# The planned delay between dependent instructions of one engine, kept for the second mixture's operations only

## The chip, the core and the metric

The kernel runs on one core of one Trainium2 chip. The metric is the device time of one execution in microseconds (us). The kernel before took 911.47 us in the median of three runs (908.46 to 913.42).

## What is computed

```python
# attention: 4 batches, 8 heads, 576 positions, head width 64, mask in blocks of 64
attn_out = _attn_ref(q, k, v)
x = attn_out.transpose(0, 2, 1, 3).reshape(2304, 512)
# first mixture
h = (x @ w1) * (x @ w2) @ w3              # 512 -> 1024 -> 1024
x = h @ w_out                             # 1024 -> 512
# second mixture
r = np.maximum(x @ w_in, 0.0)             # 512 -> 2048
return (r * r) @ w_out2                   # 2048 -> 512
```

The weights arrive as 64-bit floats and are turned into pairs of narrower numbers (a high and a low part) on the chip; each product of the mixtures is made of three products of such parts.

## The kernel before, in words

**An order worked out ahead.** The kernel doesn't issue its work as it stands in the source. Each function (`pair`, `attend`, `first_block`, `second_block`, ...) only records operations with `od.op(engine, cost, fn, reads, writes, key)`. At the end `Order.emit` (L115) plays the whole program through on paper: for each engine it holds the time at which the engine is free, and of the operations that are ready by then it takes the one with the lowest key (`min(..., key=lambda o: (o.key, o.n))`, L140). The order in which they are taken is the order of the instructions in the program. On the chip each engine then runs its list strictly in that order and waits wherever the data is not there yet. The costs change no wait on the chip; they only decide the order, and with it how many small matmuls `warm_up` (L390) puts into the gaps that PE has on paper before the first weights are ready.

An operation becomes ready when all its predecessors are done. L162 says when that is: for a successor on another engine (or a DMA) it is the end of the predecessor with its tail, plus `WAIT` of 0.03 us, plus the operation's own `spare`; for a successor on the same engine (PE, ACT or DVE) it is the time at which that engine is free plus `SAME`, which is 0 for PE, 0.125 us for ACT and 0.117 us for DVE (L83). So between two dependent instructions of DVE the paper engine has a gap of 0.117 us into which another ready operation, even of a higher key, may slip. DMA is played as one line: a transfer lands after its share of the line and `LATE` = 4.0 us (L212).

**The first part, roughly 0 to 460 us.** It holds attention and the first mixture, which run into each other. Attention goes by pairs of heads, p = 0 to 15, each with three groups g of score tiles. `pair(p)` (L555) has keys 20p + 5g. In each group: scores on PE (L587); a memset of masked places on DVE (L604); row maxima on DVE that read the same bank (L613 or L621); a DVE multiplication of the maxima (L629), all three dependent one on the other; exponentials on ACT (L646); sums to reciprocals on DVE (L659 and L663, recorded as one operation). For p below 4 the probabilities are scaled on DVE (L672), turned on PE (L730) and copied by ACT (L736). From p = 4 they are split into two f16 parts (ACT L687, DVE L694) and turned by a DMA transpose that SP issues (L704). `attend` then multiplies with v on PE (L779, or L836 for p below 4), in two parts; its keys are 20p + 16 and 20p + 17, and for p of 4 or more scores and value products have a `spare` of 2.0 us.

`convert` (L280) makes weights ready: a load issued by POOL (L304), two ACT passes over the two halves of each word (L312, L316), a DVE shift (L322), a dependent DVE add (L325), and the split into high and low (ACT L236, DVE L239). There are 29 of these in the first part (5 for `wo`, 8 for `w3`, 16 for `w12`), with keys 3 to 12, 14 to 42 and 60 to 90, among those of the pairs. `setup_rows` multiplies `w3` by `wo` on PE (`po`, L872). `v_scales` (L434) reads v a second time for b = 1 to 3 (three loads `va` of 384 KB each, L448, reduced on DVE at L453) and has keys 10, 90 and 170.

`first_block` (L950) is the first mixture: for each batch and each of two groups of tokens, 16 accumulations `ab` of 24 and then four `y` of 24 matmuls, in chunks of six (`CHUNK`, L860). Its PE keys begin at 100000, so on paper PE takes a chunk only when no attention product is ready. Its evictions (L972, L990, L236, L239, L1016) have the key -1000000 and go ahead of everything.

**The second part, roughly 460 to 910 us.** `second_block` (L1066) records everything of the second mixture: its 32 weight conversions (also through `convert`, L1249), norms, scales, and the products L1441, L1526 and L1587. The function also records the last `y` products of the first mixture.

Of the kernel before, what the change touches and what calls it, by code (L numbers as in the profile page):

```python
# [47 lines left out]
class Buf:  # L48


    def __init__(self, order, pool, tag, bufs, shape, dtype, name):
        self.order, self.pool, self.tag, self.bufs = order, pool, tag, bufs
        self.shape, self.dtype, self.name = shape, dtype, name
        line = order.lines.setdefault((pool, tag), [])
        self.before = line[-bufs] if len(line) >= bufs else None
        line.append(self)
        self.ops = []
        self.t = None
# [18 lines left out]
class Order:  # L77
# [7 lines left out]
    def __init__(self):  # L85
        self.lines, self.pools, self.ops, self.after = {}, {}, [], {}
        self.writer, self.readers = {}, {}
        self.bufs = []
        self.idle = None

    def buf(self, pool, tag, bufs, shape, dtype, name):
        b = Buf(self, pool, tag, bufs, shape, dtype, name)
        self.bufs.append(b)
        return b

    def op(self, eng, cost, fn, r=(), w=(), key=0.0, spare=0.0):

        o = Op(eng, cost, fn, key, spare)
        for k in r:
            if k in self.writer:  # L100
                o.deps.add(self.writer[k])
            self.readers.setdefault(k, []).append(o)
        for k in w:
            if k in self.writer:
                o.deps.add(self.writer[k])
            o.deps.update(self.readers.pop(k, ()))
            self.writer[k] = o
        for k in list(r) + list(w):
            if isinstance(k[0], Buf):
                k[0].ops.append(o)  # L110
        o.deps.discard(o)
        self.ops.append(o)
        return o

    def emit(self):  # L115
        for b in self.bufs:
            if b.pool in self.after:
                for o in b.ops:
                    o.deps.add(self.after[b.pool])
            if b.before is not None:  # L120
                for o in dict.fromkeys(b.ops):
                    o.deps.update(x for x in b.before.ops if x is not o)
        for o in self.ops:
            o.left = len(o.deps)
            for d in o.deps:
                d.users.append(o)
        free, avail, dma = {}, {}, 0.0
        for n, o in enumerate(self.ops):
            o.n = n
            if not o.left:  # L130
                avail.setdefault(o.eng, []).append(o)
        count = 0
        while True:
            best = None
            for eng, todo in avail.items():
                if not todo:
                    continue
                t0 = free.get(eng, 0.0)
                start = max(t0, min(o.ready for o in todo))
                o = min((o for o in todo if o.ready <= start), key=lambda o: (o.key, o.n))  # L140
                if best is None or start < best[0]:
                    best = (start, o, eng)
            if best is None:
                break
            start, o, eng = best
            if eng == "P" and self.idle:
                self.idle(start - free.get(eng, 0.0))
            avail[eng].remove(o)
            count += 1
            if isinstance(o.cost, tuple):  # L150
                issue, move, late = o.cost
                free[eng] = start + issue
                dma = max(dma, start + issue) + move
                o.end = dma + late
            else:
                free[eng] = start + o.cost
                o.end = free[eng] + self.TAIL.get(eng, 0.0)
            o.fn()
            for u in o.users:
                u.left -= 1  # L160
                same = u.eng == eng and eng in "PAV"
                u.ready = max(u.ready, free[eng] + self.SAME[eng] if same else o.end + self.WAIT + u.spare)  # L162
                if not u.left:
                    avail.setdefault(u.eng, []).append(u)
        assert count == len(self.ops), (count, len(self.ops))
# [3 lines left out]
def fused_kernel(ctx: ExitStack, tc: tile.TileContext, qT, kT, vp, va, w12, w3t, wo, wb, out):  # L169
# [4 lines left out]
    od = Order()  # L174
# [882 lines left out]
    def closing(fn, old, new):  # L1057
        close = od.op("N", 0.0, fn)
        for x in new:
            od.after[x] = close  # L1060
        for (pool_, _), line in od.lines.items():
            if pool_ in old:
                for b in line:
                    close.deps.update(b.ops)

    def second_block():  # L1066
        closing(close_attention, ("at", "ps"), ("wp", "mb"))
        closing(close_x, ("xp",), ("w2",))

# [390 lines left out]
        def combine(j, key):  # L1460
# [5 lines left out]
            def sub(o, x, y, op, r, w):  # L1466
                od.op(
                    DVE, c_dve(TH), lambda: dve.tensor_tensor(out=o(), in0=x(), in1=y(), op=op), r, w, key, S_SPARE
                )
# [199 lines left out]
    for b in range(B):  # L1669
# [17 lines left out]
        for g in range(2):  # L1687
            first_block(b, g)
    second_block()
    od.emit()  # L1690

# [50 lines left out]
```

## Time and profile before

| | |
|---|---|
| runs shown | 908.46, 911.47, 913.42 us |
| profiled execution | 912.01 us, span 910.2 us |
| mean granted clock of TensorE | 0.986 |
| busy over the span | PE 869.5 us (96%), DVE 614.0 (67%), ACT 558.5 (61%) |

The span runs from the first to the last instruction of the profiled execution; 1.8 us of its 912.01 us lie around it. "Busy" of PE is a modelled value, since matmuls are pipelined. A clock of 1.0 is 2.4 GHz, 0.5 is 1.2 GHz.

### The profile page before, as it was taken

How to read it: one execution, taken by the hardware profiler on the slowest of the kernel's cores; microseconds unless marked ns; L12 is line 12 of the kernel's file. 1: busy time of each engine (PE TensorE's matmuls, PEld its weight loads, DVE VectorE, ACT ScalarE, POOL GpSimd, SP SyncE). 2: the span in 40 equal slices, each digit the busy share in tenths (PEclk: the TensorE clock that was granted, in tenths of full speed). 3: DMA queues.
4: the chain of work that ended last, by engine and by line, in shares of the span. 5: the costliest groups of instructions: out<-in, count | busy, mean ns of one | idle time of the engine just before them, and what ended most of it. 6: DMA issues, size and time to landing. Idle time of an engine off the chain costs nothing.

```text
span 910.2 us, 18059 instructions
## 1 busy us (share of the span) xinstructions
PE 869.5 (96%) x7040; PEld 695.5 (76%) x7040; DVE 614.0 (67%) x1391; ACT 558.5 (61%) x1281; POOL 110.2 (12%) x206
## 2 busy tenths in 40 slices
PE   7799999499999999999999999999999999999997
PEld 5566678499899999999999978666666666666664
DVE  5988697467676575637368989888954484475443
ACT  6996597266674576646358898655653554454342
POOL 5112122020201002010012212000010001000000
PEclk8999999699999999999999999999999999999999
DMA  8633579798864779455626646000020002001001
GB/s 321 263 119 111 166 235 167 84 187 145 157 146 90 151 145 214 109 112 107 117 100 201 197 145 206 1 24 1 1 94 1 1 1 93 1 1 47 1 1 47
DMA packets 103990, 98.04 MB, mean 108 GB/s; under 512 B 82976, under 2 KB 86816, under 8 KB 102496
## 3 DMA queue, kind: packets, MB, share of 16 engines
q0 software_dynamic: 17888, 70.14, 24.7%
q1 hardware_dynamic: 86016, 26.75, 18.3%
q8 instruction: 55, 0.90, 0.4%
q14 instruction: 31, 0.25, 0.1%
HBM read 60.69 MB, written 9.44 MB: 77 GB/s over the span
## 4 chain that ended last, share of the span: by engine, by line
issue 39%; PE 38%; DMA 4%; ACT 2%; POOL 2%; DVE 1%; POOLq 0%; DVEq 0%; ACTq 0%
PE ab L872 20%; PE y L872 10%; PE s L587 4%; PE pv L779 4%; DMA pt<-p 3%; POOL out L1629 1%; DMA va<-in_va 1%; POOL yraw L1134 1%; ACT wb L271 1%; DMA raw<-in_w 1%; ACT raw L316 0%; ACT raw L312 0%; ACT r L1451 0%; ACT g L262 0%; DMA out<-ob 0%
## 5 line engine op out<-in xcount | busy, mean ns | idle before, releaser
L1587 PE MATMUL o<-wb,g 128*128 128x512 f16 x864 | 194.3, 379 | 0.6 <-DVE c L1597 0.6
L1587 PEld LDWEIGHTS <-g 128*128 128x128 f16 x864 | 84.5, 98 | 93.4 <-issue 0.8
L872 PE MATMUL ab<-x0h,w 128*128 128x320 f32 x512 | 120.0, 316 | 1.8 <-DVE w3o L929 1.4
L646 ACT ACTIVATE pf<-s,nm 128x192 f32<-128x192 f32 (+4 forms) x160 | 83.3, 532 | 50.7 <-DVE nm L629 41.3
L872 PE MATMUL y<-g,w3o 128*128 128x320 f32 (+1 forms) x768 | 107.1, 297 | 0.0
L872 PEld LDWEIGHTS y<-g,w3o 128*128 128x128 f32 x768 | 103.3, 188 | 2.8 <-issue 2.4
L872 PE MATMUL ab<-x1h,w 128*128 128x256 f32 x512 | 98.3, 286 | 0.0
L1414 ACT ACTIVATE c<-c,beta 128x512 f32<-128x512 f32 x64 | 45.4, 713 | 86.3 <-DVE c L1547 86.2
L872 PEld LDWEIGHTS ab<-x0h,w 128*128 128x128 f32 x512 | 87.7, 190 | 4.8 <-DVE w3o L929 1.9
L1526 PEld LDWEIGHTS <-wb 128*128 128x128 f16 x768 | 75.1, 98 | 15.8
L872 PEld LDWEIGHTS ab<-x1h,w 128*128 128x128 f32 x512 | 80.5, 188 | 2.9 <-issue 1.6
L694 DVE SCALAR_TENSOR_TENSOR p<-pf,r,p 128x192 f16<-128x192 f32 (+2 forms) x120 | 62.9, 545 | 26.8 <-ACT p L687 25.9
L872 PE MATMUL ab<-x0l,w 128*128 128x320 f32 x256 | 79.8, 312 | 0.3 <-DVE x0l L798 0.3
L264 DVE TENSOR_TENSOR g<-c,g 128x512 f16<-128x512 f32 x64 | 43.8, 690 | 50.1 <-ACT g L262 49.9
L872 PE MATMUL ab<-x1l,w 128*128 128x256 f32 x256 | 72.1, 282 | 0.0
L687 ACT ACTIVATE p<-pf,r 128x192 f16<-128x192 f32 (+2 forms) x120 | 62.0, 557 | 5.8 <-DMA pt<-p 4.1
L1526 PEld LDWEIGHTS <-st 128*128 128x128 f16 x576 | 56.3, 98 | 7.2
L587 PE MATMUL s<-kraw,qraw 64*128 64x288 f32 (+4 forms) x384 | 57.4, 423 | 2.3 <-ACT pf L646 1.6
L872 PE MATMUL po<-wo,w 128*128 128x512 f32 x192 | 51.1, 408 | 5.0 <-DVE w3o L929 2.7
L1547 DVE TENSOR_TENSOR c<-p,x 128x512 f32<-128x512 f32 x32 | 22.1, 689 | 46.0 <-PE p L1526 37.2
L236 ACT ACTIVATE g<-a 128x320 fp32r<-128x320 f32 (+1 forms) x64 | 28.3, 443 | 35.2 <-DVE a L990 35.2
L1629 POOL DMA_DIRECT2D out<-ob x18 | 9.8, 547 | 329.4 <-DVE ob L1597 294.9
(193 smaller groups left out, 1807.4 us busy)
## 6 DMA issues: line engine op xcount, KB each, us to landing
raw<-in_wb POOLq DMA_DIRECT2D x32, 512.0 KB, 5.1
raw<-in_w3t POOLq DMA_DIRECT2D x8, 1024.0 KB, 15.0
raw<-in_w POOLq DMA_DIRECT2D x16, 512.0 KB, 4.5
vraw<-in_vp POOLq DMA_DIRECT2D x16, 320.0 KB, 4.9
qraw<-in_qT POOLq DMA_DIRECT2D x16, 288.0 KB, 3.7
kraw<-in_kT POOLq DMA_DIRECT2D x32, 144.0 KB, 4.7
out<-ob POOLq DMA_DIRECT2D x18, 256.0 KB, 2.8
yraw<-ydram POOLq DMA_DIRECT2D x8, 512.0 KB, 4.9
```

What stands on the lines that cost most here:

```text
L236: od.op(ACT, c_act(n), lambda: act.activation(hi(), src(), AF.Copy), [ks], kh, key)
L264: DVE, c_dve(n), lambda: dve.tensor_tensor(out=lo(), in0=src(), in1=hi(), op=ALU.subtract), kh + ks, kl, key
L587: pe.matmul(o[:, h] if t == 4 else o, q()[rows, q_start(t) : q_start(t) + 128], keys_()[rows, c], start=True, stop=True,)
L646: act.activation(o, view(a, t), AF.Exp, bias=nm()[:, k, a : a + 1], scale=SCALE, accum_out=ssum()[:, k, a : a + 1],)
L687: lambda o=o, nk=nk, a=a, k=k, w=weights, p16=p16, r=r: act.activation(p16()[:, o : o + nk], w(a, k), AF.Copy, scale=r()[:, k, a : a + 1]),
L694: lambda o=o, nk=nk, a=a, k=k, w=weights, p16=p16, r=r: dve.scalar_tensor_tensor(out=p16()[:, o + nk : o + 2 * nk], in0=w(a, k), scalar=r( ...
L779: pe.matmul(dst, w()[:, c, hl, rows], rhs, start=n == 0, stop=n == len(steps) - 1)
L872: pe.matmul(acc(), l, r, start=k == 0, stop=k == len(mms) - 1)
L1414: lambda: act.activation(src(), src(), AF.Relu, scale=beta()[:, j, k : k + 1]),
L1526: pe.matmul(acc()[:, TH * half : TH * half + TH], lhs(a, kc), y[yn]()[:, kc], start=n == 0, stop=n == len(mms) - 1,)
L1547: DVE, c_dve(n), lambda: dve.tensor_tensor(out=o(), in0=x(), in1=y(), op=ALU.add), r, w, K_EVICT
L1587: pe.matmul(o(), g[gx]()[:, cols], wt(f)[:, a, 512:1024], start=(begin and n == 0), stop=(last and n == 2),)
```

## The change

Each operation gets its own `same` when it is recorded, taken from `od.same`. That is empty (so 0 for every engine) until `second_block` begins, where it is set to the old `SAME`. `emit` uses the successor's `same` in place of the common one.

```diff
@@ Order.__init__
         self.idle = None
+        self.same = {}
@@ Order.op
         o = Op(eng, cost, fn, key, spare)
+        o.same = self.same.get(eng, 0.0)
         for k in r:
@@ Order.emit
                 same = u.eng == eng and eng in "PAV"
-                u.ready = max(u.ready, free[eng] + self.SAME[eng] if same else o.end + self.WAIT + u.spare)
+                u.ready = max(u.ready, free[eng] + u.same if same else o.end + self.WAIT + u.spare)
@@ second_block
     def second_block():
+        od.same = od.SAME
         closing(close_attention, ("at", "ps"), ("wp", "mb"))
```

## Rows read from the trace of the kernel before

**Rows 1.** Busy time by stage: PE, PEld, DVE, ACT, POOL, then clock and DMA.

```profile
core 0: us, PE busy (x) PEld busy (x) DVE busy (x) ACT busy (x) POOL busy (x), PEclk, DMA share, GB/s
0.00:60.00 60.00, 46.56 (x383) 35.28 (x384) 48.06 (x95) 51.35 (x101) 16.82 (x35) 0.94 0.72 267
60.00:125.00 65.00, 61.43 (x415) 44.68 (x415) 51.19 (x122) 45.76 (x116) 12.99 (x24) 1.00 0.44 137
125.00:150.00 25.00, 23.59 (x157) 22.38 (x156) 23.55 (x53) 23.21 (x55) 6.47 (x12) 1.00 0.99 187
150.00:180.00 30.00, 16.05 (x110) 13.97 (x109) 12.44 (x29) 7.99 (x22) 1.08 (x2) 0.72 0.87 126
180.00:460.00 280.00, 279.71 (x2852) 259.34 (x2852) 173.93 (x452) 167.85 (x475) 35.19 (x64) 1.00 0.69 137
460.00:550.00 90.00, 90.00 (x738) 83.71 (x735) 78.15 (x193) 77.32 (x172) 19.96 (x40) 1.00 0.53 176
550.00:600.00 50.00, 47.70 (x355) 35.77 (x355) 46.84 (x114) 34.02 (x75) 6.06 (x10) 1.00 0.24 78
600.00:910.00 310.00, 304.50 (x2047) 200.34 (x2044) 179.86 (x341) 150.98 (x270) 11.60 (x20) 1.00 0.06 21
```

**Rows 2.** What PE waited for: us in total, times, longest.

```profile
PE pv L779 <- DMA pt<-p: 13.6, 2, 13.1
PE pv L836 <- DVE x0l L239: 3.1, 1, 3.1
PE tp L730 <- DVE pf L672: 2.7, 2, 2.5
PE po L872 <- DVE w3o L929: 2.7, 3, 1.3
```

**Rows 3.** The chain that ended last, around 172 us: start, us, what.

```profile
144.86 27.12 DMA pt<-p
172.29 2.12 PE s L587 x8
174.41 3.47 PE ab L872 x12
...
186.83 1.17 PE s L587 x8
188.00 6.37 PE y L872 x42
```

**Rows 4.** The DMA transposes L704 issued 140 to 165 us, then 180 to 480.

```profile
L704 SPq DMA_TRANSPOSE pt<-p x4: 1576/6226/17755, 137.0 to 162.7; - x4
DMA to landing us min/median/max: 10.2/22.3/28.1
...
L704 SPq DMA_TRANSPOSE pt<-p x66: 1232/1282/3747, 181.7 to 446.3; - x66
DMA to landing us min/median/max: 3.1/4.5/8.4
```

**Rows 5.** The loads of v for its scales, L448, 130 to 170 us.

```profile
L448 POOL DMA_DIRECT2D va<-in_va x6: 539/543/571, 138.9 to 155.6; - x6
DMA to landing us min/median/max: 12.3/16.0/19.0
```

**Rows 6.** Dependent and independent neighbours on DVE: start us, us, what.

```profile
11.19 0.17 DVE L659 TENSOR_SCALAR r<-ssum 128x4 f32<-128x4 f32 x1 [0.60 <-ACT pf L646]
11.39 0.18 DVE L663 RECIPROCAL r<-r 128x4 f32<-128x4 f32 x1
11.61 1.14 DVE L672 TENSOR_SCALAR pf<-pf,r 128x192 f32<-128x192 f32 x4
...
200.27 0.18 DVE L663 RECIPROCAL r<-r 128x4 f32<-128x4 f32 x1
200.37 0.40 DVE L990 TENSOR_TENSOR a<-ab,a 128x256 f32<-128x256 f32 x1
```

**Rows 7.** How often the dependent DVE operations of the first part occur, by line.

```profile
L629 DVE TENSOR_SCALAR nm<-nm x48: 148/168/172, 9.0 to 431.2; 128x4 f32<-128x4 f32 x32, 128x2 f32<-128x2 f32 x16
L325 DVE CUSTOM_DVE_ANT_0 cx<-raw,cx x29: 666/693/1226, 14.0 to 147.2; 128x1024 uint16<-128x1024 uint16 x18, 128x2048 uint16<-128x2048 uint16 x11
L663 DVE RECIPROCAL r<-r x48: 165/178/180, 11.4 to 434.3; 128x4 f32<-128x4 f32 x32, 128x2 f32<-128x2 f32 x16
```

**Rows 8.** DVE in order of time where others stand between dependent operations.

```profile
35.77 0.68 DVE L322 TENSOR_SCALAR cx<-raw 128x1024 int32<-128x1024 int32 x1
36.37 1.08 DVE L621 TENSOR_REDUCE nm<-s 128x2 f32<-128x896 f32 x1
37.37 1.21 DVE L325 CUSTOM_DVE_ANT_0 cx<-raw,cx 128x2048 uint16<-128x2048 uint16 x1
...
52.67 0.19 DVE L604 MEMSET s<- 64x64 f32 x2
52.77 0.68 DVE L322 TENSOR_SCALAR cx<-raw 128x1024 int32<-128x1024 int32 x1
53.37 1.40 DVE L613 TENSOR_REDUCE nm<-s 128x1 f32<-128x576 f32 x2
54.70 1.21 DVE L325 CUSTOM_DVE_ANT_0 cx<-raw,cx 128x2048 uint16<-128x2048 uint16 x1
55.83 0.16 DVE L629 TENSOR_SCALAR nm<-nm 128x2 f32<-128x2 f32 x1
...
195.87 1.29 DVE L621 TENSOR_REDUCE nm<-s 128x2 f32<-128x384 f32 x2
197.18 0.17 DVE L604 MEMSET s<- 64x128 f32 x1
197.26 0.15 DVE L629 TENSOR_SCALAR nm<-nm 128x4 f32<-128x4 f32 x1
```

## The prediction, made blind

> **What bounds the kernel now.** I read the busy time by stage first [rows 1], to see where PE has idle time that another order could give back. From 180 to 550 us PE is idle for 0.3 us of 370: here the span is the sum of PE's work, and an order that keeps PE fed can gain nothing. From 550 on it is idle for 7.8 us, 2.3 of them up to 600; that stretch belongs to the second mixture, whose operations keep the old delay. Nearly all idle time lies ahead of 180 us: 13.4 us up to 60, 3.6 to 125, 1.4 to 150 and 14.0 to 180, together 32.4 us. The change can win no more than that and what a lower clock costs there.
>
> Then the list of what PE waited for [rows 2]. One wait stands out: 13.6 us of value products for the DMA transpose of the probabilities, 13.1 of them in one piece. The others are of 1 to 3 us, for the splits of x (DVE), the scaled probabilities (DVE) and the folded weights.
>
> The chain that ended last shows that piece's place [rows 3]: a transpose issued at 144.86 us, on which everything hangs for 27.12 us. Of the transposes issued between 140 and 165 us the median landed after 22.3 us and the slowest after 28.1, while the 66 later ones took 4.5 [rows 4]. In the same stretch POOL issued six loads of v, which landed after 12.3 to 19.0 us [rows 5], at a DMA share of 0.99 from 125 to 150 us [rows 1]. So the transposes of the first pair that uses them (p = 4) met the loads. The wait has a second price. In 150 to 180 us the mean granted clock is 0.72 [rows 1], so TensorE was at 1.2 GHz for (1 - 0.72) x 30 / 0.5 = 17 us, which began while PE stood idle; of the work behind the wait, 12 `ab` matmuls took 3.47 us where 42 `y` matmuls took 6.37, or 1.82 for 12, and 8 score matmuls 2.12 where others took 1.17 [rows 3]. That is 1.65 + 0.95 = 2.6 us, and the place costs 13.6 + 2.6 = 16.2 us in all.
>
> **The change, part by part.** No instruction is added or removed, save some of the warm-up matmuls, whose number follows the paper gaps of the first microseconds; I cost these at nothing, since they run only where PE would idle. What moves is the order, wherever a dependent operation of DVE or ACT became ready 0.117 or 0.125 us late on paper and another slipped in.
>
> *How many places.* On DVE: 48 times memset to maximum and 48 times maximum to L629 (48 L629 rows), 29 times shift to add (29 L325 rows) [rows 7], and reciprocal to L672 in the 12 groups of p below 4 (of the 48 reciprocals). That is 137; the short chains of `v_scales` add a few. On ACT I found no chain of the first part in which one ACT operation directly feeds the next without DVE between them.
>
> *What the gap is on the chip.* L663 starts 0.20 us after L659, on which it depends, and L672 0.22 after L663; the independent L990 starts 0.10 after such an L663 [rows 6]. A dependent neighbour costs 0.10 to 0.12 us more, so the number taken out of the plan was about right. The Trainium skill says otherwise (VectorE: DVE Perf Modes, "The DRAIN you can't avoid"): the next Vector operation waits for the pipe to empty in any case, and a semaphore between two of them costs nothing extra. By that rule the removed delay was never there, the new order would lose nothing at any place, and the losing term below would be zero. The trace does not bear it out for these small operations.
>
> *What changes hands.* Only an operation of a higher key is displaced; evictions have the lowest key and, where ready, go first before and after. In the first 150 us I find some ten such places. The add of a `w3` conversion (key 18) came 1.0 us later because a maximum (key 25) slipped in at 36.37; at 52.77 a shift (key 34) went between a memset and its maxima (key 30), and at 54.70 its add, 1.21 us long, between the maxima and L629 [rows 8]. In the new order the lower key goes at once and DVE stands still for 0.12 us. Gain: the displaced chain is 0.6 to 1.2 us earlier. Loss: 10 x 0.12 = 1.2 us of DVE time. From 0 to 60 us ACT is busy for 51.35 and DVE for 48.06 us [rows 1]; most of these places feed ACT, which has a queue then, and between 60 and 125 us PE is idle for only 3.6 us, so an earlier softmax has little to feed. Bounds: -3 us (three places that lie ahead of a PE wait of the size in rows 2, at 1 us each) to +1.2 us. I take -0.5, near zero, since PE's waits of that stretch are spread over many causes.
>
> *From 180 us on.* Places such as 197.18, where a memset of the next group goes between maxima and L629 [rows 8], change by 0.1 us each. DVE is busy for 173.93 of 280 us and the paper spare for value products is 2.0 us, so nothing reaches PE: 0, from -0.3 (all the idle time there is) to +0.3 us. That cover is DVE's and ACT's free third; in 460 to 550 us they are busy for 78.15 and 77.32 of 90 us, but the conversions there keep the delay and the attention is over.
>
> *The wait at 158 to 172 us.* The new plan believes that p = 4's probabilities come earlier, and puts the value product earlier among the chunks of six on PE. A chunk is 6.37 / 42 x 6 = 0.91 us [rows 3]. On the chip the transposes land when DMA lets them, so each chunk that falls behind the value product adds 0.91 us of idle time. Two delays less in a group are 0.23 us, which is zero or one chunk: I take half, +0.5 us. The loads of v go out when the `w12` conversions release their buffers, and neither their number nor their keys change, so the meeting remains; its bounds are the two rivals.
>
> The sum: 912.0 (the profiled execution: 910.2 span and 1.8 around it) - 0.5 + 0 + 0.5 = 912.0; it stands 0.5 us above the median of the runs shown, so against that the forecast is **911.5 us**.
>
> **The rivals.**
> *Faster: the transposes get ahead of the loads.* The four transposes of rows 4 and the six loads of rows 5 overlap by chance of a few microseconds. If the softmax of p = 4 comes out 1 to 2 us earlier (the gain of the ten places, added up along its chain), or the loads later, the transposes land after some 10 to 18 us rather than 28, and PE's wait shrinks by about 10 us, which leaves too little idleness for the lower clock (2.6 us). That gives 911.5 - 10 = 901.5, in the extreme 911.5 - 16.2 = 895.3 us. For it: ten flips lie ahead of that point, and the wait is much longer than any other. Against it: DVE and ACT are busy for 23.55 and 23.21 of 25 us just ahead of it [rows 1], so 1 us earlier for one chain is 1 us later for the conversions, whose buffers the loads need.
>
> *Slower: the plan runs ahead of the chip.* The delays are real, so taking them out makes the paper DVE quicker than the chip's. Along the attention chain up to p = 4's second group are 14 groups with two delays, 12 scalings and 29 conversions, at most 28 x 0.117 + 12 x 0.117 + 29 x 0.117 = 8.1 us. If most are exposed on paper, the value product of p = 4 stands up to nine chunks too early, each 0.91 us of added idle time; above five chunks it is over 0.5%. Price: up to 911.5 + 8.2 = 919.7, about 917 in the middle. For it: only from p = 4 on is there a spare, and it covers 2.0 us. Against it: DVE is busy for 80% of the time up to 60 us and 94% in 125 to 150 [rows 1], so on paper too most gaps were filled, and the conversions' shift often waits for ACT anyway.
>
> *It does not do what it says.* The order could come out the same nearly everywhere; then the time is 911.5, inside the forecast. The other half of its name is sure: every conversion of the second mixture is recorded after `od.same` is set.
>
> **How the numbers follow.** Forecast 0.42, faster rival 0.32, slower rival 0.26. A measurement of this kernel can tell a difference of about 0.5%, 4.6 us, from no change (its three runs lie 5 us apart). The forecast's own range is 907 to 915. From 898 to 920 leaves out the far end of the faster rival and what lies above the slower one's price, no more than 2 in 10. Chances: faster 0.32, same 0.42, slower 0.26.
>
> **What would show it right or wrong.** Right: in the chain that ended last a DMA transpose issued near 145 us still stands for 25 us or more; PE's idle time from 180 to 550 us stays under 2 us; the stage from 600 on is alike to 1 us; L629 follows its maxima directly near 55 us. The faster rival shows as a wait for `pt` of under 6 us and a clock of 1.0 from 150 to 180 us. The slower one shows as a longer wait of L779 at the same landing, or as new waits of `po` for conversions before 60 us. I would be wrong altogether if the time moved behind 460 us, or if PE waited several microseconds for DVE between 180 and 460.

## The result, and the profile after

The changed kernel took 900.16 us in the median of four runs (897.88 to 903.67) against 910.43 us (908.46 to 913.42) before: a ratio of 0.9888, 95% interval 0.9843 to 0.9932. So it is faster by 1.1%, where the forecast was no change (911.5 us); the time lies in the range, 1.3 us from the price of the faster rival (901.5 us). The profiled execution took 901.04 us, span 899.3, mean granted clock 0.990. In the experiments below a time is the median of four or five runs (lowest to highest), and a ratio is to the kernel before on the same chip, with its 95% interval. One run, of the kernel with the delay dropped for attention alone (913.18 us), is over 1.5% above the fastest of that kernel, counts as slow and stands in none of its numbers.

The busy time by stage of the kernel after, columns as in [rows 1]:

```profile
0.00:60.00 60.00, 47.50 (x362) 36.37 (x364) 46.30 (x93) 49.51 (x98) 16.58 (x35) 0.89 0.72 267
60.00:125.00 65.00, 59.19 (x371) 43.03 (x369) 47.50 (x109) 41.80 (x104) 10.83 (x20) 0.97 0.36 111
125.00:150.00 25.00, 23.55 (x182) 21.48 (x177) 23.00 (x50) 23.98 (x58) 5.34 (x10) 1.00 0.83 236
150.00:180.00 30.00, 30.00 (x276) 27.74 (x276) 27.30 (x65) 20.71 (x55) 7.02 (x13) 1.00 0.78 176
180.00:460.00 280.00, 279.71 (x2827) 259.96 (x2826) 174.35 (x447) 167.37 (x469) 34.72 (x66) 1.00 0.71 137
460.00:550.00 90.00, 90.00 (x736) 83.76 (x735) 82.32 (x208) 81.52 (x180) 21.48 (x39) 1.00 0.57 187
...
600.00:920.00 320.00, 293.50 (x1975) 193.31 (x1973) 171.16 (x321) 142.72 (x253) 11.61 (x20) 1.00 0.06 21
```

Read line by line against [rows 1]. From 150 to 180 us PE was idle for 14.0 us at a clock of 0.72; now it is idle for none at 1.00. From 60 to 125 us its idle time rose from 3.6 to 5.8 us and the clock fell from 1.00 to 0.97; up to 60 us the idle time fell by 0.9 us but the clock went from 0.94 to 0.89. From 180 to 550 us PE's idle time stayed at 0.3 us, and in the last stage PE simply ends 11.0 us earlier (304.5 us of work left at 600 us before, 293.5 now).

An estimate from these rows closes the account. Behind the wait, at the lower clock, 12 `ab` matmuls took 3.47 us [rows 3]; in the kernel after 12 took 1.95 us at a clock of 1.00 (chain below). So I count time at 1.2 GHz as half lost: a stage loses (1 - clock) x its length beside PE's idle time. That is a little too much where PE was idle at the lower clock; for 150 to 180 us, where it was so for most of it, the prediction's 2.6 us stand instead.

| PE time lost, us | before: idle + clock | after: idle + clock |
|---|---|---|
| 0 to 60 | 13.4 + 3.6 | 12.5 + 6.6 |
| 60 to 125 | 3.6 + 0 | 5.8 + 2.0 |
| 125 to 150 | 1.4 + 0 | 1.4 + 0 |
| 150 to 180 | 14.0 + 2.6 | 0 + 0 |
| sum | 38.6 | 28.3 |

That is 10.3 us less, of a span that is 10.9 us shorter. The wait gave 16.6 us, and the stretch ahead of it took about 6 back.

What PE waited for after, over the whole span (us in total, times, longest):

```profile
PE pv L838 <- DVE x0l L241: 5.3, 2, 3.8
PE po L874 <- DVE w3o L931: 4.1, 5, 1.7
PE tp L732 <- DVE pf L674: 4.0, 3, 2.6
PE tp L732 <- ACT pt L738: 3.2, 5, 1.1
```

The 13.6 us for `pt` of [rows 2] are gone from the list. The other waits on DVE of [rows 2], for the splits of x, the scaled probabilities and the folded weights, were 3.1 + 2.7 + 2.7 = 8.5 us and are 5.3 + 4.0 + 4.1 = 13.4 us.

The chain that ended last, around p = 4's first value product (start, us, what):

```profile
133.97 16.03 PE ab L874 x108
150.01 1.17 PE s L589 x8
151.18 10.76 PE ab L874 x72
161.94 1.98 PE s L589 x16
163.92 1.95 PE ab L874 x12
165.87 1.06 PE pv L781 x28
166.94 8.12 PE y L874 x54
```

In the place of the transpose of 27.12 us [rows 3] stands PE's own work, without a gap. The DMA transposes issued from 140 to 166 us, and the loads of v from 140 to 180:

```profile
L706 SPq DMA_TRANSPOSE pt<-p x5: 1232/1679/3699, 145.6 to 165.0; - x5
...
DMA to landing us min/median/max: 3.3/6.1/8.2
```

```profile
L450 POOL DMA_DIRECT2D va<-in_va x6: 537/542/580, 146.7 to 161.3; - x6
...
DMA to landing us min/median/max: 3.4/4.4/6.2
```

The transposes land after 6.1 us in the median where it was 22.3 [rows 4], the same six loads after 4.4 us where it was 16.0 [rows 5]. The loads did not move away: in both kernels the transposes of p = 4 (issued from 134.9 us before, one start ahead of the window of [rows 4], from 145.6 us here) and the six loads (138.9 to 155.6 us, and 146.7 to 161.3) lie in one stretch. Yet now all of them pass. The DMA queues from 130 to 180 us show how differently (packets, MB, share of 16 engines' time). Before:

```profile
q0 software_dynamic: 1170, 4.85, 51.9%
q1 hardware_dynamic: 7168, 2.23, 42.4%
```

After:

```profile
q0 software_dynamic: 1828, 7.30, 46.7%
q1 hardware_dynamic: 9280, 2.75, 33.4%
```

Before, the loads (q0) and the transposes (most of q1) occupied the engines longer and moved less: MB divided by share is 9.3 in q0 against 15.6 after, and 5.3 against 8.2 in q1. Below, this state is called the jam: transposes that land late while the engines' share is high and the rate low.

### The profile page after: what moved, and what is told of

It reads as the page before. It is cut to its first block, busy times and chain, and to the rows that moved or that the text cites. A ratio compares the mean times of both kernels' runs of the same rounds, so it can differ in the third digit from the quotient of the medians.

```text
span 899.3 us, 18055 instructions
## 1 busy us (share of the span) xinstructions
PE 871.2 (97%) x7036; PEld 697.7 (78%) x7036; DVE 616.6 (69%) x1391; ACT 559.8 (62%) x1281; POOL 109.9 (12%) x206
## 4 chain that ended last, share of the span: by engine, by line
PE 42%; issue 38%; ACT 2%; POOL 1%; DVE 1%; DMA 1%; POOLq 0%; DVEq 0%; ACTq 0%
PE ab L874 23%; PE y L874 10%; PE s L589 4%; PE pv L781 4%; POOL yraw L1137 1%; DMA out<-ob 1%; POOL out L1632 1%; ACT wb L273 1%; ACT raw L318 0%; ACT raw L314 0%; ACT r L1454 0%; PE pv L838 0%; ACT g L264 0%; PE nq L1281 0%; ACT r L1420 0%
## 5 line engine op out<-in xcount | busy, mean ns | idle before, releaser
L874 PE MATMUL po<-wo,w 128*128 128x512 f32 x192 | 54.2, 430 | 5.5 <-DVE w3o L931 4.1
L874 PEld LDWEIGHTS po<-wo,w 128*128 128x128 f32 x192 | 37.1, 203 | 16.7 <-DVE w3o L931 7.5
```

The source lines that it names most:

```text
L874: pe.matmul(acc(), l, r, start=k == 0, stop=k == len(mms) - 1)
```

## The experiments

**The theory**: the whole gain is the jam, which the new order happens to avoid; dropping the delay gains nothing anywhere else. **Rivals**: the gain comes from the shorter delay as such (DVE and ACT get to the critical work sooner); or from one half of the changed operations, conversions or attention.

### The jam taken out of the kernel before

```diff
-                GQ, c_dma(384), lambda s=src, v=view: pool.dma_start(out=v(), in_=s), [], [(raw,)],
+                GQ, c_dma(384), lambda s=src, v=view: pool.dma_start(out=v(), in_=s),
+                [("pt", 8 * b - 8 + a, 2) for a in range(2)] if b > 1 else [], [(raw,)],
```

This goes into the kernel before, with the old delay everywhere. On paper the loads of v for b = 2 and 3 now come behind the last transposes of p = 4 (b = 2) and p = 8 (b = 3), so they move back in POOL's list. It is an order alone: no wait on the chip is added.

> The kernel before, with the old delay everywhere; only the six loads of v for the scales of batches 2 and 3 wait until the last transposes of the first pair of the batch before are done. Theory 1 (the long wait at 158 to 172 us is a meeting of DMAs: the transposes and copies of p = 4 fall among the last weight loads and these six loads): the transposes issued near 143 and 145 us land after under 12 us rather than 28, PE's wait for them falls from 13.6 to under 3 us, and the time comes to 893 to 902 us without any change of the delay. Rival A (the copies and the weight loads alone make the jam, the loads of v only sit in it): the transposes still take over 18 us and the time stays above 906. Rival B (the gain has to do with the order on PE or DVE, not with DMA): the time stays at 909 to 914 even if the loads go.

897.04 us (895.03 to 897.59), ratio 0.9821 (0.9802 to 0.984) to the kernel before on its chip (913.5). Two loads still left early, at 145 us, and the third at 167. Its transposes:

```profile
L705 SPq DMA_TRANSPOSE pt<-p x4: 1232/1868/4615, 135.9 to 145.7; - x4
...
DMA to landing us min/median/max: 5.3/7.3/8.5
```

and its stage of the old wait:

```profile
150.00:180.00 30.00, 30.00 (x278) 27.35 (x277) 23.30 (x56) 17.77 (x48) 4.34 (x8) 1.00 0.78 157
```

Moving four loads, with the delay untouched, gives 16.5 us (913.5 - 897.0), as much as the 16.2 us at which the prediction priced the place, and more than the change itself. So the wait was worth that much, and in the order of the kernel before the loads were a condition of it.

### Half of those loads moved

The same edit, so that only the three loads for b = 3 move:

```diff
-                [("pt", 8 * b - 8 + a, 2) for a in range(2)] if b > 1 else [], [(raw,)],
+                [("pt", 8 * b - 8 + a, 2) for a in range(2)] if b > 2 else [], [(raw,)],
```

> The kernel before; of the six loads of v only the three for batch 3 wait, the three for batch 2 go out as before, two ahead of and one just behind the second group's transposes. Theory 1 in its simple form (bytes in front of the transposes): the jam is about half as long, transposes land after 12 to 20 us, 899 to 907 us. If the jam starts with the first loads and feeds itself: as before, over 20 us and 908 to 914. If it needs all six: under 9 us and 895 to 899.

903.12 us (902.46 to 906.28), ratio 0.9913 (0.9882 to 0.9945). The transposes, and what PE waited for:

```profile
L705 SPq DMA_TRANSPOSE pt<-p x4: 1425/3576/10992, 137.4 to 147.2; - x4
...
DMA to landing us min/median/max: 9.3/15.9/18.7
```

```profile
PE pv L780 <- DMA pt<-p: 5.0, 2, 4.4
```

In the kernel before the jam has a dose. With six loads beside it the slowest transpose took 28.1 us and PE waited 13.6; with three, 18.7 and 5.0; with two, 8.5 and not at all. The times follow, as ratios to the kernel before on each chip: 1, 0.9913, 0.9821.

### The same gate in the changed kernel

The edit of the first experiment, made in the kernel after.

> The changed kernel with the same gate on the six loads of v as in e1. Theory 1 (all that the change gains is that the transposes and those loads no longer jam): with the gate in both, the change has nothing left to give, so this run is within 4 us of e1's 897, 893 to 901 us. Rival (the new order is also better in itself, by the shorter attention chain): below 890 us. Rival (the old delay is the better plan once the jam is gone): above 901.

900.28 us (898.85 to 900.73), ratio 0.9883 (0.9844 to 0.9921), as without the gate. Where the jam is gone already, moving the loads gains nothing; the two changes are one gain, not two.

### Half of the change: conversions alone, attention alone

```diff
     od = Order()
+    od.same = od.SAME
...
         n_raw[0] += 1
+        od.same = od.SAME if home else {}
...
         split(hi, lo, lambda: x().bitcast(F32), n, (kh, kl, (xb,)), key)
+        od.same = od.SAME
```

So only the conversions of the first part lose the delay. The other kernel keeps it there, and sets `od.same = {}` around `pair` and `attend` instead.

> One part of the change alone: in the first part the delay is dropped only for the operations of the weight conversions and kept for attention. Theory 1: what matters is whether p = 4's copies are issued before or after the last of the 16 w12 loads. In this order they come after it, so the transposes land within 12 us, there is no wait of over 3 us at that place, and the time is 896 to 905 us. Rival B (the shorter attention chain is what gains): 908 to 914, with the long wait still there.

> The other part alone: the delay is dropped only for attention's operations and kept for the conversions. Theory 1: here too p = 4's copies come after the last w12 load, so there is no long wait and the time is 896 to 905 us, although nothing is common with the run before but that order. Rival B (only one of the two parts holds the gain): this run and the one before differ by more than 6 us.

Conversions alone: 901.05 us (896.55 to 908.81), 0.9891 (0.9829 to 0.9954), the slowest of its transposes 8.4 us, no wait of PE for one. Attention alone: 904.0 us (898.88 to 907.7, three runs), 0.9896 (0.9849 to 0.9943), with half a jam:

```profile
L707 SPq DMA_TRANSPOSE pt<-p x6: 1469/3828/8004, 141.7 to 164.8; - x6
...
DMA to landing us min/median/max: 7.4/10.8/17.5
```

```profile
PE pv L782 <- DMA pt<-p: 5.2, 1, 5.2
```

The first came out as expected; the second missed on the wait, which was not to be there. Both are faster than the kernel before, so neither half alone holds the gain. Their runs spread over 12 and 9 us, so the two can't be ranked. Of the two profiled executions the one without the wait took 898.1 us and the one with it 904.0; whether the slower runs of each had a jam is not shown.

### Other sizes of the delay

Half of it in the first part, and 1.25 of it, in place of none:

```diff
+    od.same = {"A": 0.0625, "V": 0.0585}
```

```diff
+    od.same = {"A": 0.156, "V": 0.146}
```

> Half the delay in the first part (0.0585 us on DVE, 0.0625 on ACT). If the gain came from the size of the delay, half of it would give half the gain: 905 to 907 us. Theory 1: the size means nothing, the order it happens to give means all; in this order p = 4's copies stand among the last four w12 loads again, as in the kernel before, so the transposes take over 15 us and the time is 906 to 916 us.

> The old delay made a quarter longer in the first part (0.146 us on DVE, 0.156 on ACT). On paper it gives nearly the order of the kernel before around the transposes: copies with the last loads, transposes 1 us behind, loads of v among them. Theory 1: the jam is there again, transposes over 15 us, and the time is 907 to 916 us. Rival (a delay that is too long or too short costs in proportion, by idle time on paper): 912 to 918 with a jam or without.

Half: 901.18 us (899.6 to 901.88), 0.9868 (0.985 to 0.9886). 1.25: 899.06 us (897.3 to 900.8), 0.9867 (0.9832 to 0.9903). Neither has the wait. Both expectations missed: by the paper order the copies of p = 4's v stood among the loads of the last `w12` parts, as before, and I had taken that for the sign of a jam. It isn't: at about the same share of the DMA engines, half the delay moves 319 GB/s where before moved 67. In slices of 5 us (columns as in [rows 1]), half the delay:

```profile
145.00:150.00 5.00, 5.00 (x36) 4.33 (x34) 4.41 (x12) 5.00 (x16) 0.54 (x1) 1.00 1.11 319
```

and in the next 10 us, where the loads of v left:

```profile
150.00:155.00 5.00, 5.00 (x34) 5.00 (x35) 5.00 (x14) 5.00 (x12) 2.38 (x4) 1.00 1.12 280
155.00:160.00 5.00, 5.00 (x36) 5.00 (x35) 5.00 (x11) 3.04 (x7) 1.09 (x2) 1.00 1.11 234
```

The kernel before, whose loads of v left from 138.9 us on:

```profile
145.00:150.00 5.00, 5.00 (x36) 5.00 (x36) 5.00 (x12) 3.21 (x7) 1.12 (x2) 1.00 1.15 67
```

A longer delay than the original gains as much as none at all. With none, 0.5, 1 and 1.25 of the delay the times are 900, 901, 912 and 899 us: the size is not what pays. Of these four only the original value sets up the full jam. The rival that the shorter delay pays as such falls here.

### The jam put back into the changed kernel

A first try made the last four `w12` loads depend, on paper alone, on the split of v for p = 4 (`loads` collects the loads as they are recorded):

```diff
+        if p == 4:
+            for o in loads[25:29]:
+                o.deps.add(od.ops[-1])
```

> The changed kernel, with the last four of the 16 w12 loads held until p = 4's split of v is done, so that they are issued together just ahead of its copies and transposes, which the new order had kept apart. Theory 1: the jam is put back: the first four transposes land after more than 12 us, PE waits for them for over 4 us, and the time is 905 to 920 us. Rival (the order on DVE and ACT holds the gain): the transposes may be slow, but the time stays at 897 to 903.

903.33 us (899.21 to 904.83), 0.9902 (0.9868 to 0.9935). It tells nothing of the jam: on the chip the four loads still left at 133 to 139 us, ahead of the copies of v at 141. A dependency of the plan that is no wait on the chip only orders a queue, so neither side of the expectation was tested. The second try gives POOL an instruction that really reads the data:

```diff
         whole = [(t, x, a) for x in "hl" for a in range(2)]
+        if p == 4:
+            hold = at_buf("hold", 1, [P, 1], F16, "hold")
+            o = od.op(GQ, 0.2, lambda: pool.tensor_copy(out=hold(), in_=t()[:, 0, 1, 64:65]), whole, [(hold,)], key)
+            for x in loads[25:29]:
+                x.deps.add(o)
```

> The changed kernel with one more POOL instruction, a copy of one column of p = 4's split v, ahead of the last four w12 loads: now they really wait on the chip until that split is done (in e6 the order on paper alone held them, and they left early). They are then issued within 3 us together with the copies, just ahead of the transposes, as in the kernel before. Theory 1: the first four transposes land after more than 12 us, PE waits over 3 us for them and the time is 904 to 920 us. Rival: the transposes land within 9 us and the time is 897 to 904.

913.55 us (909.92 to 922.35, ten runs), 1.0025 (0.9996 to 1.0054): the gain is gone. The four loads left together at 144.6 to 146.2 us, and the transposes were jammed again:

```profile
L712 SPq DMA_TRANSPOSE pt<-p x4: 1852/5461/7557, 146.0 to 160.7; - x4
...
DMA to landing us min/median/max: 14.3/18.6/19.0
```

The stage, and the slice in which the rate collapses:

```profile
150.00:180.00 30.00, 26.24 (x174) 23.74 (x175) 21.80 (x48) 18.85 (x48) 5.14 (x10) 0.89 1.15 199
...
160.00:165.00 5.00, 2.83 (x20) 2.57 (x18) 0.61 (x2) 0.20 (x1) 0.54 (x1) 1.00 1.49 95
```

But the wait came by another road than expected. PE did not wait for `pt` itself, which the expectation had. ACT did, for 6.1 us, before it could split the next probabilities, and the split of a `w12` part stands behind it in ACT's list, for which PE then waited. What ACT waited for from 140 to 185 us, and PE from 150 to 185:

```profile
ACT p L695 <- DMA pt<-p: 6.1, 1, 6.1
```

```profile
PE ab L880 <- ACT w L238: 3.5, 2, 3.3
```

By the estimate of the section on the result PE loses 3.8 + 3.3 (clock 0.89 over 30 us) = 7.1 us here where the kernel after loses none, and 1.35 us more from 180 to 460 us; up to 60 us it loses another 1.4. The sum, 9.8 us, is what the last stage ends later (303.28 us against 293.50 from 600 us on). One reserve: POOL stood still for 8 us before the added copy, so the held loads are themselves 6 to 10 us late and the loads of v behind them 7 us (from 154.1 us on). ACT waited 1.2 us for one held load. I take most of the price as the jam's, but this run alone could not carry the theory.

### The gate at another place, in both kernels, on one chip

```diff
-                [("pt", 8 * b - 8 + a, 2) for a in range(2)] if b > 1 else [], [(raw,)],
+                [("pt", 8 * b - 6 + a, 2) for a in range(2)] if b > 1 else [], [(raw,)],
```

Against the first experiment, the loads now come behind the last transposes of p = 5 (b = 2) and p = 9 (b = 3). It goes into the kernel before and into the kernel after, so that neither has the jam and only the delay differs.

> The kernel before, old delay everywhere, with the loads of v for batches 2 and 3 placed in POOL's queue only behind the last transposes of the second pair of the batch before (p = 5 and 9), so that none of them is near p = 4's transposes. Theory 1: no wait of PE for transposes over 2 us, 893 to 899 us.

> The changed kernel with the same placing. With the jam away from both, this run against the one before it on the same chip is the change by itself. From e1 and e5 (0.9821 and 0.9883 of the kernel before): the dropped delay by itself costs 2 to 6 us, through longer waits of PE before 125 us (splits of x, w3o, scaled probabilities: 16.6 us together in the changed kernel, 11.1 before), so 897 to 903 us and 0.2 to 0.7% above e9. Rival (the change is neutral apart from the jam): within 1.5 us of e9. Rival (it gains by itself): more than 1.5 us under e9.

With the old delay 896.83 us (894.27 to 898.12), ratio 0.9819 (0.9794 to 0.9844); with the change 901.81 us (899.5 to 902.02), ratio 0.9875 (0.9854 to 0.9896), both to 912.0 us. The ranges of the five runs each do not meet. So with the jam out of both, the change costs 5.0 us, as expected. The kernels with the old delay and a gate (this one, and that of the first experiment at 0.9821) are the fastest of all. That the 5.0 us come from the delay being shorter is not shown: a quarter more of it, without a jam and without a gate, stands at 0.9867, no nearer to them than the change. The two profiled executions lie 3.8 us apart (898.12 and 901.93 us). Their stages up to 125 us, first with the old delay, then with the change:

```profile
0.00:60.00 60.00, 46.38 (x354) 36.22 (x354) 45.30 (x90) 48.40 (x95) 16.43 (x35) 0.89 0.72 267
60.00:125.00 65.00, 60.58 (x403) 43.65 (x404) 49.99 (x117) 44.68 (x112) 11.57 (x22) 1.00 0.38 120
```

```profile
0.00:60.00 60.00, 49.39 (x350) 37.88 (x352) 45.58 (x89) 48.95 (x97) 16.45 (x35) 0.83 0.73 266
60.00:125.00 65.00, 59.23 (x369) 43.02 (x367) 47.41 (x111) 41.78 (x103) 10.82 (x20) 0.97 0.34 108
```

Idle time and clock together lose 13.6 + 6.6 + 4.4 = 24.6 us with the old delay and 10.6 + 10.2 + 5.8 + 2.0 = 28.6 us with the change, 4.0 more; the last stage ends 3.9 us later (294.22 us against 290.34). Of this the part from 60 to 125 us repeats: PE's idle time there is 5.8 us in all five kernels with the changed plan (the kernel after, the two gated ones and the two in which loads were held) and 3.6 to 4.4 us in the four with the old one. The clock of that part is 0.97 in four of the five and 1.00 in the four with the old plan. The clock up to 60 us does not repeat: 0.83 to 0.94 with the change, 0.89 to 0.94 without. So some 1.4 to 4 us of the cost are shown in their place, from 60 to 125 us; the rest is in the runs' times but not located.

## Why the prediction was wrong, step by step

**What bounds the kernel** was right. All that could be won lay ahead of 180 us, the wait of 13.6 us with its 2.6 us of low clock was the one large piece, and its price of 16.2 us was met by the kernel in which only loads were moved (16.5 us).

**The step that failed** is the last of the parts, on the wait at 158 to 172 us: "The loads of v go out when the `w12` conversions release their buffers, and neither their number nor their keys change, so the meeting remains". The premise holds, six loads with the same keys, and even the meeting remains, in the same stretch. What does not follow is the wait, which the sum left standing with its low clock: 16.6 us before by the account above, nothing after, with transposes that landed after 8.2 us at most where it had been 28.1. Loads, copies and transposes that meet need not jam: three of the four sizes of the delay that were run escape it. The step took the meeting for the jam, and so a coincidence for a fixture; the prediction had even come near it, under the faster rival ("overlap by chance of a few microseconds"), and weighed it at 0.32.

**The half chunk** on that wait (+0.5 us) had the wrong sign as an order. Ahead of p = 4's first value product the trace before has 180 `ab` matmuls and, from 100 us on, 24 of scores; the trace after has 192 (108, 72 and 12 in the chain above) and 40. The product moved back by two chunks, not forward by one. PE reaches it at 165.8 us instead of 157.2. That did not hide the transposes: counted from them, PE comes no later, 11.0 us behind the start of p = 4's fourth (154.8 us) where it was 12.3 (144.9 us). It is the shorter landing that took the wait away, as in the kernel with the gated loads and the old delay.

**The first 150 us** (-0.5 us, bounds -3 to +1.2) were mis-sized and of the wrong sign: about +6 us in the account above; the pair on one chip has +5.0 us in all, of which its traces show 4.0 up to 125 us. The place near 55 us came out as described. L629, now L631, follows its maxima at once where a `w12` add had stood between [rows 8]; DVE in order of time, after:

```profile
54.98 1.42 DVE L615 TENSOR_REDUCE nm<-s 128x1 f32<-128x576 f32 x2
56.44 0.17 DVE L631 TENSOR_SCALAR nm<-nm 128x2 f32<-128x2 f32 x1
56.52 0.70 DVE L324 TENSOR_SCALAR cx<-raw 128x1024 int32<-128x1024 int32 x1
```

What the term left out is, first, that a new order at ten places makes new waits of PE at others: for the folded weights, from 60 to 125 us, 3.2 us where it was 1.4, and for the splits of x 5.3 us where it was 3.1. The prediction counted DVE's 0.12 us per place and not what stands behind a later split. Still, PE's idle time up to 125 us grew by only 1.3 us in all (17.0 to 18.3 us). The larger part, 5.0 of the 6.3 us of the account, is the clock, which the term had at nothing: 0.89 for 0.94 up to 60 us, 0.97 for 1.00 up to 125. After, the granted clock was 0.51 from 35 to 45 us, the lower level, behind 5 us of which PE had been busy for 2.07. Up to 60 us the clock differs like that between kernels of either plan; only what lies behind 60 us repeats with the change.

**From 180 us on** (0 us) was right: 0.3 us of idle time from 180 to 460 us before and after.

**The rivals.** The faster one named the right place, and its signs came: no wait for `pt`, clock 1.00 from 150 to 180 us. That its price of 901.5 us lies so near the 900.16 measured is in part luck: it took 10 us off at that place and nothing elsewhere, where the account has 16.6 us off and about 6 put back ahead of it. Its reason is not what happened. The softmax did not come out 1 to 2 us earlier; p = 4's first transpose left at 145.6 us, 10.7 us later than before (134.9). The loads of v left later too, but by less: the first one 1.1 us behind that transpose, where it had been 4.1. The transposes did not get ahead of the loads; they met them and passed. Its chance was too low by the argument against it, that DVE and ACT are full just ahead of the place; with three of three other sizes of the delay free of the wait, any reordering should have counted as a likely way out. The slower rival was half right: the early part did get slower, but by waits for the splits of x and the folded weights and by the clock, not by chunks ahead of a value product. Whether the cause is its own, that the dropped delay is real on DVE, is not shown: half the delay gave yet other waits (9.4 us for the folded weights) at the same total time.

On that delay the prediction had set [rows 6] against the Trainium skill (VectorE: DVE Perf Modes, "The DRAIN you can't avoid"), by which removing it would lose nothing at any place. The same section of the Trainium skill adds that a next operation that is not held starts earlier, which the prediction left out. The independent L990 of [rows 6] agrees with that: it starts 0.10 us after the start of an operation of 0.18. The pair on one chip decides nothing here: it loses 5.0 us, but by a whole new order and not by the delay itself.

**What stays open** is why a meeting jams. In the order of the kernel before it takes the loads of v beside p = 4's copies and transposes (the dose), and four held `w12` loads bring it back where it was gone. But neither the order on paper nor the share of the DMA engines tells beforehand.

## What to carry to other kernels

When a planner's constant is changed and the time moves, run a neutral change of the same kind (the constant a quarter larger) before crediting the constant: here it gained 1.3%, where the change gained 1.1%. Look in the trace for the one place where bursts of loads meet transposes that the bounding engine needs, and move the loads that nobody waits for out of it; two lines did that here for 1.8%. A dependency that exists only in the plan moves an instruction in its queue, not in time; where the time matters, the instruction must read something.

## What the runs showed of the hardware that was not expected

- A stretch in which DMA transposes and loads meet can run at a share of 1.15 and move 67 GB/s (before, 145 to 150 us), or at 1.11 to 1.12 and move 234 to 319 (half the delay, 145 to 160 us). A high share of the DMA engines does not mean that they are moving much.
- In the jam the loads suffer with the transposes: 16.0 us against 4.4 for the same 384 KB.
- A jam that PE doesn't wait for directly can still reach it through another engine's list: ACT stood 6.1 us for a transpose with a split behind it that PE needed.
